# Attention's second-head scaling and output copies moved from VectorE to ScalarE in tiles 0 and 1 of a fused attention and two-MLP kernel

## The chip, the cores and the metric

The kernel runs on one core of a Trainium2 chip. The metric is device time in microseconds, the median of several runs. Engines are named as in the profile: PE (TensorE matmuls), PEld (its weight loads), DVE (VectorE), ACT (ScalarE), POOL (GpSimd), SP (SyncE, which here only issues transfers).

## What is computed

Attention over 4 batches, 8 heads, 512 local and 32 global positions with 64 features a head; local queries see the 32 global keys and a window of 32 keys to either side. Two MLPs follow on the 2176 x 512 result (the weights have 2048 and 1536 hidden columns).

```python
s_ll = np.where(mask, scale * q_l @ k_l.T, -1e9)      # mask: |i - j| <= 32
a_l = sm(concat([scale * q_l @ k_g.T, s_ll]))         # sm: softmax over keys
out_l = a_l @ concat([v_g, v_l])
out_g = sm(scale * q_g @ k_all.T) @ v_all
x = concat([out_g, out_l]) as (tokens, 512)
h = x @ w_in
x = where(h >= 1, h, where(h <= -1, 0, (h + 1)**2 / 4)) @ w_out
out = ((x @ w_a) * (x @ w_b)) @ w_out2
```

## The kernel before

Tokens are worked in six tiles (`TILES`). Tiles 0 to 4 hold three blocks of 128 local queries each, tile 5 the last block and the global queries. One attention **item** (`Local`) is one block and one pair of heads, so a tile of three blocks has 12 items. An item goes through these steps, and the line numbers are those of the profile:

- `s_pe` (L186): scores of the two heads on PE into PSUM. Tiles 0 and 1 (blocks 0 to 5, `stk` false) multiply plain fp32; later blocks (`stk` true) split the operands first (`prep`, L166 to L169).
- `s_post` (L199, L203): DVE adds the mask and finds the row minimum, ACT takes the exponential of each head and its row sum.
- `norm` (L207 to L210): DVE adds 1e-9 to the sums and inverts them; ACT scales the first head's probabilities (L209), DVE the second head's (L210).
- `t_pe`, `t_post` (L216, L220): four PE transposes into one PSUM tile `tp`, which ACT copies to `pt`.
- `v_pe`, `v_post` (L226, L230): eight PE matmuls with the values into PSUM tile `o`, and DVE copies `o` to a slice of `xraw`, the tile's input to the MLP.

`att_atoms` runs the items as a pipeline: step k takes the scores of item k, `norm` of k-1, the transposes of k-2, the values of k-3. All 12 items of tile 0 run first, alone. This is **the opening**. Every eighth piece of it, one weight of the first MLP is converted (`w_conv`, L97 on ACT and L98 to L100 on DVE; `split`, L107 on ACT and L108 on DVE). Four weights are converted in the opening, and the first two steps of tile 1's pipeline fall into it too.

After it `x_split` makes `xh` (ACT, L405) and `xl` (DVE, L406) of tile 0, and the first MLP starts. For each of 16 hidden slices of a tile `h_unit` multiplies into PSUM `hp` (L423 to L425), ACT and DVE make `r`, `m`, `g` (L703 to L709), and `x_unit` accumulates into four `acc` banks. During **tile 0's MLP** (in the profile about 44 to 150 us) the 12 items of tile 1 run between these units, and the other 28 weights of the first MLP are converted. In the MLPs of tiles 1 to 3 the next tile's items and the second MLP's weights are worked; the second MLP comes last.

Work is written in this order, but it is a scheduling pass that places each engine's instructions into its queue; each engine then runs its own queue strictly in order, and waits on semaphores. `e`, `mn` and `sm` have four buffers, PSUM's eight banks are split into four of tag `h` (scores, `hp`) and four of tag `acc` (`tp`, `o` of tile 0, `acc`).

Of the kernel before, what the change touches and what calls it, by code (L numbers as in the profile page):

```python
# [14 lines left out]
AF = mybir.ActivationFunctionType  # L15
# [4 lines left out]
P = 128  # L20
# [38 lines left out]
def body(tc, qk, qkd, vw, kg, vg, w1i, w1o, w2a, w2b, w2o, mask, out):  # L59
    nc = tc.nc  # L60
# [75 lines left out]
    xraw_cur = {}  # L136
# [6 lines left out]
    class Local:  # L143
# [62 lines left out]
        def norm(self):  # L206
            nc.vector.tensor_scalar_add(self.sm, self.sm, 1e-9)  # L207
            nc.vector.reciprocal(self.sm, self.sm)
            nc.scalar.activation(self.e[:, 0], self.e[:, 0], AF.Copy, scale=self.sm[:, 0:1])  # L209
            nc.vector.tensor_scalar_mul(self.e[:, 1], self.e[:, 1], self.sm[:, 1:2])  # L210

        def t_pe(self):
            self.tp = ps.tile([P, 4, P], F32, name="tp", tag=self.tag)
# [13 lines left out]
                                     self.pt[:KC, 2 * c + h], start=c == 0, stop=c == 1)  # L227

        def v_post(self):
            nc.vector.tensor_copy(xraw_cur[self.t][self.p][:, self.j * P:(self.j + 1) * P], self.o)  # L230

    class Gap:
        stk = False
# [674 lines left out]
```

## Time and profile before

| | us |
|---|---|
| median of 3 runs | 957.22 |
| lowest and highest | 955.91, 957.3 |
| the profiled execution | 954.88 |
| its span, first to last instruction | 953.1 |

| stretch of the profiled execution | us |
|---|---|
| first exponential on ACT to the first `xh` (the opening) | 5.36 to 37.21 |
| TensorE clock at its lower level | about 37.0 to 43.6 |
| tile 0's MLP at full clock, tile 1's items in it | 44 to 150 |
| tiles 1 to 3 | 150 to about 430 |

Busy time of an engine counts the time in which at least one of its instructions runs. Back to back instructions of ACT and DVE overlap a little, so what one costs in a full queue is the distance to the next one's start, not its own duration. A wait names what ended it last. The chain of waits follows the work that ended last backwards.

### The profile page before, as it was taken

How to read it: one execution, taken by the hardware profiler on the slowest of the kernel's cores; microseconds unless marked ns; L12 is line 12 of the kernel's file. 1: busy time of each engine (PE TensorE's matmuls, PEld its weight loads, DVE VectorE, ACT ScalarE, POOL GpSimd, SP SyncE). 2: the span in 40 equal slices, each digit the busy share in tenths (PEclk: the TensorE clock that was granted, in tenths of full speed). 3: DMA queues.
4: the chain of work that ended last, by engine and by line, in shares of the span. 5: the costliest groups of instructions: out<-in, count | busy, mean ns of one | idle time of the engine just before them, and what ended most of it. 6: DMA issues, size and time to landing. Idle time of an engine off the chain costs nothing.

```text
span 953.1 us, 16713 instructions
## 1 busy us (share of the span) xinstructions
PE 926.9 (97%) x5964; PEld 840.3 (88%) x5964; DVE 728.2 (76%) x1881; ACT 539.6 (57%) x1293; POOL 0.7 (0%) x7
## 2 busy tenths in 40 slices
PE   7898988999999999999999999999999999999997
PEld 5587777999999999987889999999999999999996
DVE  6799999888877877764348968888896666877663
ACT  8867767666666666654445555555654444654441
POOL 0000000000000000000000000000000000000000
PEclk9899999999999999999999999999999999999999
DMA  7455546444544444333454323321241111131201
GB/s 238 148 189 182 182 164 188 156 133 142 178 142 132 160 156 147 96 120 104 134 194 149 94 79 112 98 69 48 72 147 45 45 45 48 44 121 56 57 12 56
DMA packets 55843, 111.49 MB, mean 117 GB/s; under 512 B 6864, under 2 KB 23376, under 8 KB 55760
## 3 DMA queue, kind: packets, MB, share of 16 engines
q1 hardware_dynamic: 55616, 110.26, 36.4%
q8 instruction: 47, 0.77, 0.3%
q14 instruction: 36, 0.29, 0.1%
q10 hardware_dynamic: 144, 0.17, 0.1%
HBM read 95.20 MB, written 15.20 MB: 116 GB/s over the span
## 4 chain that ended last, share of the span: by engine, by line
PE 84%; DVE 9%; ACT 3%; DMA 2%; issue 1%; SPq 0%; ACTq 0%; DVEq 0%
PE hp L423 6%; PE hp L425 6%; PE hp L424 6%; PE acc L423 6%; PE acc L424 5%; PE acc L425 5%; PE pb L580 5%; PE pb L581 5%; PE py L645 5%; PE pb L578 5%; PE py L646 5%; PE py L644 5%; PE px L578 4%; PE px L581 4%; PE px L580 4%; PE o L226 3%
## 5 line engine op out<-in xcount | busy, mean ns | idle before, releaser
L423 PE MATMUL hp<-xh,w 128*128 128x384 f32 (+1 forms) x384 | 131.5, 342 | 5.4 <-ACT xh L405 2.1
L423 PE MATMUL acc<-g,w 128*128 128x384 f32 (+1 forms) x384 | 132.0, 344 | 4.2 <-ACT g L708 3.6
L424 PE MATMUL acc<-g,w 128*128 128x384 f32 (+1 forms) x384 | 127.1, 331 | 0.0
L425 PE MATMUL hp<-xl,w 128*128 128x384 f32 (+1 forms) x384 | 126.5, 330 | 0.0
L424 PE MATMUL hp<-xh,w 128*128 128x384 f32 (+1 forms) x384 | 126.0, 328 | 0.0
L425 PE MATMUL acc<-g,w 128*128 128x384 f32 (+1 forms) x384 | 125.0, 330 | 0.0
L107 ACT ACTIVATE w<-wt 128x512 fp32r<-128x512 f32 (+1 forms) x116 | 64.9, 564 | 70.8 <-PE pb L581 44.9
L580 PE MATMUL pb<-w 128*128 128x384 f32 (+1 forms) x288 | 94.7, 329 | 0.0
L581 PE MATMUL pb<-w 128*128 128x384 f32 (+1 forms) x288 | 94.3, 327 | 0.0
L578 PE MATMUL pb<-w 128*128 128x384 f32 (+1 forms) x288 | 93.7, 325 | 0.0
L704 DVE SCALAR_TENSOR_TENSOR m<-hp,r 128x384 f32<-128x384 f32 (+1 forms) x96 | 51.1, 532 | 49.5 <-ACT r L703 49.4
L703 ACT ACTIVATE r<-hp,half 128x384 f32<-128x384 f32 (+1 forms) x96 | 53.4, 556 | 61.1 <-PE hp L425 60.6
L423 PEld LDWEIGHTS hp<-xh,w 128*128 128x128 f32 x384 | 72.9, 190 | 12.8 <-issue 3.4
L423 PEld LDWEIGHTS acc<-g,w 128*128 128x128 f32 x384 | 72.4, 189 | 12.5 <-issue 5.3
L645 PE MATMUL py<-w,g 128*128 128x512 f32 x204 | 80.8, 396 | 0.0
L646 PE MATMUL py<-w,g 128*128 128x512 f32 x204 | 80.7, 396 | 0.0
L644 PE MATMUL py<-w,g 128*128 128x512 f32 x204 | 79.6, 390 | 0.0
L108 DVE TENSOR_TENSOR w<-wsum,w 128x256 fp32r<-128x256 f32 (+1 forms) x108 | 54.6, 507 | 29.6 <-ACT w L107 29.6
L424 PEld LDWEIGHTS acc<-g,w 128*128 128x128 f32 x384 | 72.6, 189 | 1.6 <-issue 1.0
L425 PEld LDWEIGHTS acc<-g,w 128*128 128x128 f32 x384 | 72.2, 188 | 1.7 <-issue 1.2
L708 ACT ACTIVATE g<-m 128x384 fp32r<-128x384 f32 (+1 forms) x96 | 48.3, 503 | 44.6 <-DVE m L705 43.9
L425 PEld LDWEIGHTS hp<-xl,w 128*128 128x128 f32 x384 | 72.9, 190 | 0.7 <-DVE xl L406 0.5
(112 smaller groups left out, 2131.6 us busy)
## 6 DMA issues: line engine op xcount, KB each, us to landing
wt<-wd SPq DMA_DIRECT2D x72, 256.0 KB, 2.7
qkd<-in_qkd_dram SPq DMA_DIRECT2D x40, 352.0 KB, 3.1
wraw<-in_w1i_dram SPq DMA_DIRECT2D x16, 512.0 KB, 3.5
wraw<-in_w1o_dram SPq DMA_DIRECT2D x16, 512.0 KB, 4.0
v<-in_vw_dram SPq DMA_DIRECT2D x64, 112.0 KB, 2.8
wraw<-in_w2a_dram SPq DMA_DIRECT2D x12, 512.0 KB, 3.7
wraw<-in_w2b_dram SPq DMA_DIRECT2D x12, 512.0 KB, 4.0
wd<-wt SPq DMA_DIRECT2D x24, 256.0 KB, 2.2
```

The source lines that it names most:

```text
L107: nc.scalar.activation(hi, src, AF.Copy)
L108: nc.vector.tensor_tensor(lo, src, f32(hi), ALU.subtract)
L423: nc.tensor.matmul(acc, whi, xhi, start=first, stop=False)
L424: nc.tensor.matmul(acc, wlo, xhi, start=False, stop=False)
L425: nc.tensor.matmul(acc, whi, xlo, start=False, stop=last)
L578: nc.tensor.matmul(out[:, :n], w[:, 0, r], hi[:, c, :n], start=start and c == 0, stop=False, skip_group_check=True)
L580: nc.tensor.matmul(out[:, :n], w[:, 1, r], hi[:, c, :n], start=False, stop=False, skip_group_check=True)
L581: nc.tensor.matmul(out[:, :n], w[:, 0, r], lo[:, c, :n], start=False, stop=k in (1, 5, 6) and c == 1, skip_group_check=True)
L644: nc.tensor.matmul(a, gh[:, c], w[:, 0], start=f == 0, stop=False)
L645: nc.tensor.matmul(a, gh[:, c], w[:, 1], start=False, stop=False)
L646: nc.tensor.matmul(a, gl[:, c], w[:, 0], start=False, stop=f == NF2 - 1)
L703: at["act"] = nc.scalar.activation(r[:, :W], hp[:, :W], AF.Relu, bias=half, scale=0.5 / W_UP).ins
```

## The change

In `norm` the second head's scaling, and in `v_post` the copy of `o` to `xraw`, go to ACT where `stk` is false, that is for all 24 items of tiles 0 and 1. Later items keep DVE. Nothing else in the code differs.

```diff
@@ norm
             nc.scalar.activation(self.e[:, 0], self.e[:, 0], AF.Copy, scale=self.sm[:, 0:1])
-            nc.vector.tensor_scalar_mul(self.e[:, 1], self.e[:, 1], self.sm[:, 1:2])
+            if self.stk:
+                nc.vector.tensor_scalar_mul(self.e[:, 1], self.e[:, 1], self.sm[:, 1:2])
+            else:
+                nc.scalar.activation(self.e[:, 1], self.e[:, 1], AF.Copy, scale=self.sm[:, 1:2])
@@ v_post
-            nc.vector.tensor_copy(xraw_cur[self.t][self.p][:, self.j * P:(self.j + 1) * P], self.o)
+            x = xraw_cur[self.t][self.p][:, self.j * P:(self.j + 1) * P]
+            if self.stk:
+                nc.vector.tensor_copy(x, self.o)
+            else:
+                nc.scalar.activation(x, self.o, AF.Copy)
```

In the changed file the scaling on ACT is L213, `pt` is L223, the copy on ACT L237, `xh` L412, `hp` L430 to L432, and `m` L711 and L712. The scheduling pass places all queues anew up to the start of tile 1's MLP; behind it they stand as before.

ACT's queue, the end of the opening before: `e` are probabilities, `mn` and `sm` row minima and sums, `xh_625` is the first input of the MLP.

```order
L220 ACTIVATE pt<-tp 112x512
L203 ACTIVATE e,sm<-e,mn 128x224
L107 ACTIVATE w<-wt 128x512
L203 ACTIVATE e,sm<-e,mn 128x224
L209 ACTIVATE e<-e,sm 128x224
L220 ACTIVATE pt<-tp 112x512
L405 ACTIVATE xh_625<-xraw_223 128x384
```

The same place after:

```order
L223 ACTIVATE pt<-tp 112x512
L107 ACTIVATE w<-wt 128x512
L237 ACTIVATE xraw_225<-o 128x128
L203 ACTIVATE e,sm<-e,mn 128x224 x2
L209 ACTIVATE e<-e,sm 128x224
L213 ACTIVATE e<-e,sm 128x224
L223 ACTIVATE pt<-tp 112x512
L237 ACTIVATE xraw_226<-o 128x128
L412 ACTIVATE xh_625<-xraw_223 128x384
```

Each turn of the pipeline now has a second scaling (L213) and an output copy (L237) in ACT's queue, and the last copy stands ahead of `xh`. The queue up to `xh` holds the same 30 exponentials, 13 `pt` copies and four weights (L97, L107) as before, and in addition 14 scalings and 12 copies.

DVE's queue in tile 0's MLP before, from the inversion of one item's sums: `wt`, `wraw` and `w` belong to a weight's conversion, `m`, `g` and `hp` to the MLP.

```order
L207 TENSOR_SCALAR sm<-sm 128x2
L108 TENSOR_TENSOR w<-wt,w 128x512
L208 RECIPROCAL sm<-sm 128x2
L709 TENSOR_TENSOR g<-m,g 128x384
L210 TENSOR_SCALAR e<-e,sm 128x224
L230 COPY xraw_770<-o 128x128
L98 TENSOR_SCALAR wt<-wt 128x512 x2
L99 SCALAR_TENSOR_TENSOR wt<-wraw,wt 128x512 x2
L100 SCALAR_TENSOR_TENSOR wt<-wraw,wt 128x512 x2
L704 SCALAR_TENSOR_TENSOR m<-hp,r 128x384
```

The same place after:

```order
L207 TENSOR_SCALAR sm<-sm 128x2
L108 TENSOR_TENSOR w<-wt,w 128x512
L208 RECIPROCAL sm<-sm 128x2
L716 TENSOR_TENSOR g<-m,g 128x384
L98 TENSOR_SCALAR wt<-wt 128x512
L711 SCALAR_TENSOR_TENSOR m<-hp,r 128x384
L99 SCALAR_TENSOR_TENSOR wt<-wraw,wt 128x512
L98 TENSOR_SCALAR wt<-wt 128x512
```

The item's scaling (L210) and copy (L230) are gone from DVE's queue, and `m` of the next `hp` (L704, now L711) stands behind one conversion instruction where it stood behind six.

## Rows read from the trace of the kernel before

**Rows 1.** Page, parts 1 and 4: busy per engine; the chain by engine.
```profile
PE 926.9 (97%) x5964; PEld 840.3 (88%) x5964; DVE 728.2 (76%) x1881; ACT 539.6 (57%) x1293; POOL 0.7 (0%) x7
...
PE 84%; DVE 9%; ACT 3%; DMA 2%; issue 1%; SPq 0%; ACTq 0%; DVEq 0%
```

**Rows 2.** Stretches: busy us (instructions) of each engine, granted TensorE clock, DMA.
```profile
core 0: us, PE busy (x) PEld busy (x) DVE busy (x) ACT busy (x) POOL busy (x), PEclk, DMA share, GB/s
5.36:37.21 31.85, 26.99 (x218) 18.32 (x216) 27.95 (x131) 30.78 (x96) 0.00 (x0) 1.00 0.75 229
...
44.00:150.00 106.00, 96.23 (x574) 81.47 (x574) 103.38 (x255) 72.06 (x157) 0.00 (x0) 1.00 0.54 178
150.00:240.00 90.00, 88.36 (x579) 81.33 (x579) 75.25 (x221) 62.20 (x164) 0.00 (x0) 1.00 0.48 153
```

**Rows 3.** Chain of waits in the opening, 5 to 37.3 us: shares by line.
```profile
by line: DMA qk<-in_qk_dram 16.6%; PE s L186 15.0%; DVE e L199 10.7%; PE tp L216 10.4%; PE o L226 9.2%; DVE wt L99 5.5%; DVE xraw L230 5.1%; issue 4.2%; DVE e L210 4.1%; DVE wt L100 3.9%; DVE w L108 3.7%; PE warm L191 2.0%; DVE wt L98 2.0%;
```

**Rows 4.** ACT groups, opening: count, busy us, mean ns, idle before.
```profile
L203 ACT ACTIVATE e<-e,mn 128x224 f32<-128x224 f32 x30 | 14.1, 470 | 3.4 <-DVE mn L199 3.2
L220 ACT ACTIVATE pt<-tp 112x512 f32<-112x512 f32 x13 | 7.5, 578 | 0.0
L209 ACT ACTIVATE e<-e,sm 128x224 f32<-128x224 f32 x14 | 6.6, 475 | 0.4 <-DVE sm L208 0.3
L203 ACT ACTIVATION_READ_ACCUMULATOR e<-e,mn 128x1 f32 x30 | 5.7, 189 | 0.0
L97 ACT ACTIVATE wt<-wraw 128x512 f32<-128x512 f32 x4 | 2.6, 666 | 0.0
L107 ACT ACTIVATE w<-wt 128x512 fp32r<-128x512 f32 x4 | 2.5, 622 | 0.2
```

**Rows 5.** ACT timeline, one item and a half: start, duration.
```profile
23.07 0.47 ACT L209 ACTIVATE e<-e,sm 128x224 f32<-128x224 f32 x1
23.45 0.58 ACT L220 ACTIVATE pt<-tp 112x512 f32<-112x512 f32 x1
23.92 0.48 ACT L203 ACTIVATE e<-e,mn 128x224 f32<-128x224 f32 x1
24.30 0.20 ACT L203 ACTIVATION_READ_ACCUMULATOR e<-e,mn 128x1 f32 x1
24.39 0.48 ACT L203 ACTIVATE e<-e,mn 128x224 f32<-128x224 f32 x1
```

**Rows 6.** ACT groups of the whole span: PSUM copies of other sizes.
```profile
L728 ACT ACTIVATE x<-acc 128x384 f32<-128x384 f32 x12 | 5.6, 488 | 2.5 <-PE acc L425 2.5
L728 ACT ACTIVATE x<-acc 128x256 f32<-128x256 f32 x4 | 1.3, 390 | 0.0
L300 ACT ACTIVATE ptg<-tpg 32x128 f32<-32x128 f32 x8 | 2.1, 265 | 4.9 <-PE og L309 4.8
```

**Rows 7.** DVE timeline in the opening: the two operations that are moved.
```profile
15.25 0.33 DVE L210 TENSOR_SCALAR e<-e,sm 128x224 f32<-128x224 f32 x1
15.50 0.29 DVE L230 COPY xraw<-o 128x128 f32<-128x128 f32 x1
15.70 0.38 DVE L199 CUSTOM_DVE_ANT_0 e<-s,masks 128x224 f32<-128x224 f32 x1
```

**Rows 8.** DVE groups, 44 to 150 us.
```profile
L100 DVE SCALAR_TENSOR_TENSOR wt<-wraw,wt 128x512 int32<-128x512 int32 x29 | 19.5, 686 | 0.0
L210 DVE TENSOR_SCALAR e<-e,sm 128x224 f32<-128x224 f32 x10 | 3.3, 332 | 0.0
L230 DVE COPY xraw<-o 128x128 f32<-128x128 f32 x12 | 3.3, 284 | 0.0
```

**Rows 9.** Chain that ended last: first and last moved pieces on it.
```profile
71.28 0.24 DVE e L210
71.53 0.20 DVE xraw L230
...
125.22 0.20 DVE xraw L230
```

**Rows 10.** Waits, 44 to 150 us: us in total, times, longest.
```profile
ACT wt L97 <- DMA wraw<-in_w1o_dram: 4.4, 5, 1.7
PE acc L423 <- ACT g L708: 3.3, 3, 1.7
PE hp L423 <- DVE m L704: 2.0, 3, 1.0
```

**Rows 11.** PE timeline: one item, and the end of the opening.
```profile
27.05 0.65 PE L216 MATMUL tp<-ident,e 128*112 128x128 f32 x4
27.62 0.66 PE L226 MATMUL o<-pt,v 112*64 112x128 f32 x8
28.21 0.65 PE L186 MATMUL s<-qk 64*128 64x224 f32 x4
28.79 0.65 PE L216 MATMUL tp<-ident,e 128*112 128x128 f32 x4
...
34.97 0.66 PE L226 MATMUL o<-pt,v 112*64 112x128 f32 x8
37.77 0.69 PE L423 MATMUL hp<-xh,w 128*128 128x384 f32 x1 [2.14 <-ACT xh L405]
```

**Rows 12.** Stretches of 1 us around the opening's end; the clock is PEclk.
```profile
36.00:37.00 1.00, 0.00 (x0) 0.00 (x0) 0.94 (x3) 1.00 (x4) 0.00 (x0) 0.99 0.54 111
37.00:38.00 1.00, 0.23 (x1) 0.23 (x2) 0.59 (x2) 1.00 (x3) 0.00 (x0) 0.50 0.95 386
43.00:44.00 1.00, 1.00 (x4) 0.50 (x2) 0.00 (x0) 0.58 (x2) 0.00 (x0) 0.60 0.00 0
```


## Prediction

> **What bounds the kernel now.** I read the page first. PE is busy 97% of the span and the chain of waits is 84% PE [rows 1], so an edit on DVE and ACT can only show where PE stands still. That is before 150 us. The table of stretches divides this part in two [rows 2].
>
> In the opening, from the first exponential to the first `xh`, ACT is busy 30.78 of 31.85 us, DVE 27.95, PE 26.99. ACT idles 1.07 us in all: it is the bound, although the chain there walks mostly over transfers, PE and DVE [rows 3]. A chain names one predecessor at each step, and with three engines this full it can walk on any of them; what decides is who has no time left. The MLP can't start before `xh`, and `xh` stands at the end of ACT's queue.
>
> In tile 0's MLP, 44 to 150 us, it is turned round: DVE is busy 103.38 of 106 us, PE 96.23, ACT 72.06 [rows 2]. DVE's load is mostly weight conversion: L100 alone has 29 instructions and 19.5 us [rows 8]. PE has 9.8 us of idle time there, some of it waiting for DVE's `m` (2.0 us) or for `g`, which follows `m` (3.3 us) [rows 10]. From 150 us on DVE falls to 84% and PE is at 98% (75.25 and 88.36 of 90 us) [rows 2], and no queue is changed there; what is won or lost earlier is carried to the end.
>
> So the edit takes work from the bound of the second stretch and gives it to the bound of the first.
>
> **The opening, more work for ACT.** ACT's queue up to `xh` gets 14 scalings (12 items of tile 0 and the first two of tile 1) and 12 copies; all else in it is the same in number. A scaling on ACT is seen: L209 has 475 ns mean [rows 4], but in a full queue the next instruction starts 0.38 us after it (23.07 to 23.45) [rows 5]. 14 x 0.38 = 5.3 us. A 128x128 copy from PSUM on ACT is not in the trace. The nearest rows are 128x384 at 488 ns, 128x256 at 390 ns and 32x128 at 265 ns [rows 6]. 98 ns less for 128 columns less gives 292 ns for one alone; with the overlap of 0.1 us that [rows 5] show it takes 0.19 us in a full queue. 12 x 0.19 = 2.3 us. Alone, behind a wait for PE, it would be 12 x 0.29 = 3.5 us. I take the full queue, since ACT is the engine that is late: the values of item k-3 stand in PE's queue right behind the transposes of k-2, and both wait for scalings that ACT did a turn earlier. Together 7.6 us, 8.8 with copies alone.
>
> What of it can hide? Only ACT's 1.07 us of idle time. The floor is 7.6 - 1.1 = 6.5 us, and it is a hard one as long as instructions keep their durations: 30.78 + 7.6 = 38.4 us of work have to go through ACT before `xh`. I take 7.5, idle time as now, because the waits at the start (for the first scores, whose `qk` transfers are the same) and the round trips remain. DVE loses 14 scalings and 12 copies in the opening, 0.25 and 0.20 us each by the distances of [rows 7], some 5.9 us, and this buys nothing: DVE wasn't last.
>
> The Trainium skill ("ScalarE: Activation LUTs", Rules for kernel authors) advises VectorE over ScalarE for adds and multiplications, which speaks against this change. The rows agree: a scaling takes 0.38 us of ACT's queue [rows 5] and 0.25 us of DVE's [rows 7]. The same page (What ACT_TABLE_LOAD costs) gives 186 ns + 0.833 ns an element for an ACTIVATE with constants, less 93 ns back to back; by that, as an estimate, a copy is 0.20 us and the 12 are 2.4 in place of 2.3 us, and no run here shows it for 128 columns yet.
>
> **Tile 0's MLP, less work for DVE.** All 12 copies of tile 1 and 9 of its scalings fall here (10 L210 are in the stretch, one belongs to tile 2) [rows 8]: 12 x 0.20 + 9 x 0.25 = 4.65 us off an engine that is 97.5% busy. Upper bound of the gain: 4.65 us, all of it. Lower bound: only the moved pieces on which the chain of waits walks, which are six from 71.28 to 125.22 us and sum to 1.5 us [rows 9]. Neither is nearer: DVE is full, but PE with 96.23 of 106 us is the next bound close behind, and where PE ends a wait, DVE's time is worth nothing. I take the middle, 3.1 us. ACT gets 9 x 0.38 + 12 x 0.19 to 0.29 = 5.7 to 6.9 us there, on 72.06 of 106 us. That is hidden by its idle time. If it isn't, it is because a copy that waits for `o` at the head of ACT's queue keeps `r`, `g` and the next weight's L97 waiting behind it; that would eat the gain, down to zero.
>
> **The clock at the seam.** The granted clock is 0.99 at 36 to 37 us, 0.50 from 37 on and back in the 44th microsecond [rows 12], after PE had worked its last values at 34.97 and then waited 2.14 us for `xh` [rows 11]. So 6.6 us run at 1.2 GHz in place of 2.4, and cost about 3.3 us, before and presumably after: the wait for `xh` stays, as two exponentials, two scalings, a `pt` and a copy still stand between the last values and `xh`. I put the change at 0, between -3.3 (it doesn't fall) and +1.4. The latter is a second fall inside the opening. One item's transposes, values and scores take PE 0.58 us each by the starts of [rows 11], 1.75 us together, at half clock 3.5; ACT then needs 38.4 / 14 = 2.74 us an item. In 6.6 us PE would do 1.9 items where ACT could do 2.4, half an item or 1.4 us lost.
>
> "TensorE: Matmul & The Clock Gate" (Part 1: The HAM clock gate) of the Trainium skill says that an idle PE loses its full clock and a busy one gets it back. This trace shows both at the seam; by that rule the longer opening, with PE at 27 of some 39 us, would be more open to a second fall, which is the +1.4 above.
>
> **The sum.** +7.5 - 3.1 + 0 = +4.4 us. The profiled execution took 954.88 us with a span of 953.1, so it would become 959.3. It lies 2.3 us under the median of the runs; on that median, 957.22 us, I predict **961.6 us**.
>
> **Rivals.**
> - *Tile 0's MLP gives back all that the opening takes* (not slower). The place is DVE's queue from 44 to 150 us. If DVE alone is the bound, it is worth 4.65 us and the 2.6 us for which DVE idles now, since the new order puts `m` ahead of conversions: 7.3 us against 7.5, so 957.4 us. For it: DVE's 97.5%, and PE's 9.8 us of idle time, enough room. Against it: PE would have to run at 97% there, with items and MLP competing. It decides if the stretch from the first `hp` to tile 1's MLP gets shorter by over 6 us. Chance 0.13.
> - *The clock doesn't fall at the seam.* 957.2 + 4.4 - 3.3 = 958.3 us. For it: the wait that precedes the fall depends on a few instructions. Against: PE idles more in the new opening, not less. Chance 0.07.
> - *ACT isn't the bound in the opening*, its added work hides and only DVE's gain remains: 957.2 - 3.1 = 954.1 us, faster. The chain, which walks little over ACT there, speaks for it; 1.07 us of idle time against 7.6 us of work speaks against it. Chance 0.06.
> - *Nothing is given back, and the copies wait.* Opening +8.8, a second fall of the clock +1.4, MLP 0: 967.4 us. Chance 0.12.
>
> **How the numbers follow.** The forecast has 0.62: with 6.5 to 8.8 for the opening and 1.5 to 4.65 given back it runs from 959.1 to 964.5. Opening at its floor, full gain and part of the clock's gain reach down to 957.0; opening at 8.8, 1.5 given back and a second fall reach up to 965.9. That is the range, and it leaves out the faster case and the upper end of the heavy one. A change of 0.2%, 1.9 us, is about what a measurement of this kernel can tell from none. Slower by more than that: the forecast and the heavy case, 0.74, less a little for the forecast's lower edge, 0.72. Faster: 0.07. The rest, the give-back and the clock, is within 0.2%: 0.21.
>
> **What would show it.** Right: the first `xh` at 43.7 to 46 us in place of 37.21; ACT over 95% busy ahead of it with DVE at about 22 us of work; copies on ACT near 0.29 us long. In tile 0's MLP, DVE's busy time some 4.7 us less, and the stretch from the first `xh` to the start of tile 1's MLP shorter by 1.5 to 4.7 us. Wrong: `xh` before 42 us, which would say that ACT had room or that its instructions run faster; or a stretch behind it that is shorter by more than 6 us; or a clock that stays at 1.00 around the seam; or half clock for long inside the opening.

## The result and the profile after

| | before | after |
|---|---|---|
| median, us | 956.57 | 968.75 |
| lowest and highest, us | 954.97, 957.3 | 966.7, 971.21 |
| ratio | | 1.013, 95% interval 1.0102 to 1.0158 |
| the profiled execution, its span, us | 954.88, 953.1 | 966.7, 964.9 |

The kernel became slower by 12.2 us, where 4.4 were forecast. The two profiled executions differ by 11.8 us in span, and their traces place the difference so ("MLP" is the time from the first `xh` to DVE's first copy of a finished `acc` bank of tile 0, L730 before and L737 after, to 0.04 us):

| us | before | after | difference | forecast |
|---|---|---|---|---|
| first `xh` | 37.21 | 48.42 | +11.2 | +7.5 |
| tile 0's MLP | 108.74 | 109.51 | +0.8 | -3.1 |
| the rest | 807.15 | 806.97 | -0.2 | 0 |

Stretches of the trace after, which answer [rows 2]: busy time (instructions) of each engine, granted clock, DMA. They are the opening, the clock's low stretch behind it, and the rest of tile 0's MLP:

```profile
core 0: us, PE busy (x) PEld busy (x) DVE busy (x) ACT busy (x) POOL busy (x), PEclk, DMA share, GB/s
5.67:48.42 42.75, 35.49 (x218) 23.07 (x216) 22.92 (x104) 37.59 (x121) 0.00 (x0) 0.80 0.56 175
48.42:55.50 7.08, 6.49 (x17) 4.75 (x18) 3.71 (x9) 4.50 (x12) 0.00 (x0) 0.53 0.03 11
55.50:157.93 102.43, 93.79 (x560) 78.87 (x559) 95.87 (x222) 75.28 (x170) 0.00 (x0) 1.00 0.54 173
```

The same two parts of the MLP in the trace before:

```profile
37.21:44.00 6.79, 6.23 (x16) 4.56 (x16) 3.55 (x9) 3.82 (x10) 0.00 (x0) 0.51 0.17 66
44.00:145.95 101.95, 92.74 (x558) 79.03 (x557) 99.50 (x242) 69.56 (x150) 0.00 (x0) 1.00 0.53 174
```

Three things are to be seen. First, in the opening ACT is busy 6.8 us longer than in [rows 2], but the opening is 10.9 us longer, and ACT now idles 5.2 us. Second, the granted clock there is 0.80, where it was 1.00. Third, in the MLP DVE loses 3.6 us of work (99.50 to 95.87), and yet the stretch doesn't get shorter: it takes 102.43 us in place of 101.95.

**The clock in the opening.** "Half clock" is time at TensorE's lower level, 1.2 GHz in place of 2.4, which the rows show as 0.50. Stretches of 1 us of the trace after:

```profile
23.00:24.00 1.00, 0.13 (x4) 0.00 (x0) 0.23 (x2) 1.00 (x3) 0.00 (x0) 1.00 0.82 252
24.00:25.00 1.00, 0.27 (x1) 0.30 (x2) 0.00 (x0) 1.00 (x4) 0.00 (x0) 0.65 0.80 239
...
34.00:35.00 1.00, 1.00 (x10) 0.72 (x10) 0.11 (x1) 1.00 (x5) 0.00 (x0) 0.73 0.47 145
...
41.00:42.00 1.00, 0.19 (x3) 0.12 (x2) 0.56 (x4) 1.00 (x4) 0.00 (x0) 0.69 0.00 0
...
54.00:55.00 1.00, 1.00 (x3) 0.55 (x3) 0.00 (x0) 0.34 (x1) 0.00 (x0) 0.50 0.00 0
```

The rows between the first two and the third, and between the fourth and the fifth, stand at 0.50. Twice the shortfall of each row from 1.00 gives the time at the lower level: 10.2 us in the first spell, 13.6 in the second, 17.3 of the 23.9 ahead of the first `xh`. Before, [rows 12] had one spell of 6.8 us in all, behind the opening. PE's timeline shows how the first spell begins:

```profile
22.47 0.66 PE L229 MATMUL o<-pt,v 112*64 112x128 f32 x8
24.73 1.08 PE L186 MATMUL s<-qk 64*128 64x224 f32 x2 [1.60 <-DMA qk<-in_qk_dram]
25.74 1.10 PE L219 MATMUL tp<-ident,e 128*112 128x128 f32 x4
```

PE waits 1.60 us for a `qk` transfer, and then the four transposes that took 0.65 us in [rows 11] take 1.10. Who suffers is in the waits of 5.67 to 48.42 us (us in total, times, longest):

```profile
DVE e L199 <- PE tp L219: 8.0, 4, 3.7
...
ACT w L107 <- DVE wt L100: 3.6, 2, 1.9
```

and in the timelines of DVE and of ACT in that spell:

```profile
26.98 0.39 DVE L199 CUSTOM_DVE_ANT_0 e<-s,masks 128x224 f32<-128x224 f32 x1 [3.72 <-PE tp L219]
...
28.67 0.69 DVE L100 SCALAR_TENSOR_TENSOR wt<-wraw,wt 128x512 int32<-128x512 int32 x1
```

```profile
29.39 0.63 ACT L107 ACTIVATE w<-wt 128x512 fp32r<-128x512 f32 x1 [1.92 <-DVE wt L100]
29.93 0.26 ACT L237 ACTIVATE xraw<-o 128x128 f32<-128x128 f32 x1
```

DVE stands 3.72 us before an item's mask: PE stood still for 1.60 us of it, for the transfer, and then did the scores and the transposes at half clock. The weight's conversion (L98 to L100) stands behind that mask in DVE's queue, so it comes late, and ACT, which does L107 between two items, stands 1.92 us before it with an output copy and the next exponentials queued behind. The same happens once more three us behind the spell, with the clock full again:

```profile
37.42 0.63 ACT L107 ACTIVATE w<-wt 128x512 fp32r<-128x512 f32 x1 [1.68 <-DVE wt L100]
```

So 3.6 of ACT's 5.2 us of idle time are at L107. What they show is a late PE that takes time from an ACT that has none to give. How much of the lateness is the clock, the transfer or the order of the queues, these waits alone don't say.

**What the moved instructions cost.** ACT's groups in 5.67 to 48.42 us, beside [rows 4], and two rows of its timeline:

```profile
L213 ACT ACTIVATE e<-e,sm 128x224 f32<-128x224 f32 x14 | 6.7, 476 | 0.0
...
L237 ACT ACTIVATE xraw<-o 128x128 f32<-128x128 f32 x12 | 3.2, 268 | 0.4 <-PE o L229 0.4
L107 ACT ACTIVATE w<-wt 128x512 fp32r<-128x512 f32 x4 | 2.5, 629 | 3.6 <-DVE wt L100 3.6
```

```profile
13.64 0.26 ACT L237 ACTIVATE xraw<-o 128x128 f32<-128x128 f32 x1
13.80 0.47 ACT L209 ACTIVATE e<-e,sm 128x224 f32<-128x224 f32 x1
```

A copy takes 268 ns (292 were estimated) and 0.16 us of a full queue (0.19 estimated). The scalings are as [rows 4] and [rows 5] had L209. The copies hardly wait for `o`: 0.4 us in all.

### The profile page after: what moved, and what is told of

The parts are those of the page before. It is cut to its first block, busy times and chain, and to the rows that moved or that the text cites. A ratio compares the mean times of both kernels' runs of the same rounds, so it can differ in the third digit from the quotient of the medians.

```text
span 964.9 us, 16733 instructions
## 1 busy us (share of the span) xinstructions
PE 936.5 (97%) x5964; PEld 844.9 (88%) x5964; DVE 719.5 (75%) x1833; ACT 553.2 (57%) x1341; POOL 0.7 (0%) x7
## 3 DMA queue, kind: packets, MB, share of 16 engines
q1 hardware_dynamic: 55616, 110.26, 36.3%
## 4 chain that ended last, share of the span: by engine, by line
PE 84%; ACT 5%; DVE 5%; DMA 4%; issue 1%; SPq 0%; ACTq 0%; DVEq 0%
PE hp L430 6%; PE acc L430 6%; PE acc L431 6%; PE hp L432 6%; PE hp L431 6%; PE acc L432 5%; PE pb L587 5%; PE pb L588 5%; PE py L652 5%; PE pb L585 5%; PE py L653 5%; PE py L651 5%; PE px L585 4%; PE px L587 4%; PE px L588 4%; PE o L229 3%
## 5 line engine op out<-in xcount | busy, mean ns | idle before, releaser
L430 PE MATMUL acc<-g,w 128*128 128x384 f32 (+1 forms) x384 | 131.2, 343 | 5.7 <-ACT g L715 4.9
L430 PE MATMUL hp<-xh,w 128*128 128x384 f32 (+1 forms) x384 | 131.5, 342 | 3.5 <-ACT xh L412 2.1
L432 PE MATMUL hp<-xl,w 128*128 128x384 f32 (+1 forms) x384 | 126.7, 330 | 0.0
L432 PE MATMUL acc<-g,w 128*128 128x384 f32 (+1 forms) x384 | 124.9, 330 | 0.0
L107 ACT ACTIVATE w<-wt 128x512 fp32r<-128x512 f32 (+1 forms) x116 | 65.1, 564 | 70.0 <-PE pb L588 44.9
L711 DVE SCALAR_TENSOR_TENSOR m<-hp,r 128x384 f32<-128x384 f32 (+1 forms) x96 | 51.1, 532 | 48.4 <-ACT r L710 48.2
L430 PEld LDWEIGHTS acc<-g,w 128*128 128x128 f32 x384 | 72.3, 189 | 12.8 <-ACT g L715 6.9
L430 PEld LDWEIGHTS hp<-xh,w 128*128 128x128 f32 x384 | 72.9, 190 | 11.0 <-issue 3.6
L431 PEld LDWEIGHTS acc<-g,w 128*128 128x128 f32 x384 | 72.5, 189 | 3.0 <-issue 2.0
L108 DVE TENSOR_TENSOR w<-wt,w 128x512 fp32r<-128x512 f32 (+1 forms) x116 | 70.0, 606 | 6.4 <-ACT w L107 5.0
L432 PEld LDWEIGHTS hp<-xl,w 128*128 128x128 f32 x384 | 72.9, 190 | 0.8 <-DVE xl L413 0.7
```

The lines of the kernel that those rows point to most:

```text
L107: nc.scalar.activation(hi, src, AF.Copy)
L108: nc.vector.tensor_tensor(lo, src, f32(hi), ALU.subtract)
L430: nc.tensor.matmul(acc, whi, xhi, start=first, stop=False)
L431: nc.tensor.matmul(acc, wlo, xhi, start=False, stop=False)
L432: nc.tensor.matmul(acc, whi, xlo, start=False, stop=last)
```

## The experiments

Two questions had to be told apart. Where do the opening's 11.2 us come from: ACT's added work, or PE's lower clock, or the `qk` transfer that sets it off? And is DVE the bound of tile 0's MLP, so that work taken from it is won? The table has all runs. Half clock is worked out from rows of 1 us as above. The ratio is to the kernel before, run beside each; the rounds ran on different chips, so kernels of different rounds are compared by their ratios. The columns from the first `xh` on come from one profiled execution of each kernel; "fill" is explained below.

| kernel | median us | ratio (95%) | first `xh` | half clock ahead of it | MLP | half clock in it | DVE busy in it |
|---|---|---|---|---|---|---|---|
| before | | | 37.21 | 0.2 | 108.74 | 6.6 | 103.05 |
| after | 968.75 | 1.0130 (1.0102 to 1.0158) | 48.42 | 17.3 | 109.51 | 6.6 | 99.58 |
| tile 0 alone | 967.74 | 1.0116 (1.0090 to 1.0143) | 45.70 | 12.4 | 113.00 | 11.5 | 102.81 |
| tile 1 alone | 957.47 | 1.0009 (0.9993 to 1.0026) | 38.41 | 0 | 112.69 | 13.6 | 99.65 |
| after, `qk` earlier | 968.41 | 1.0118 (1.0089 to 1.0148) | 45.59 | 9.3 | 115.81 | 21.5 | 99.83 |
| after, fill | 960.69 | 1.0041 (1.0023 to 1.0058) | 43.38 | 0 | 108.35 | 6.8 | 99.62 |
| tile 0 alone, fill | 958.23 | 1.0023 (1.0011 to 1.0035) | 43.35 | 0 | 106.00 | 0 | 102.58 |
| before, fill | 954.97 | 0.9986 (0.9970 to 1.0001) | 34.46 | 0 | 111.19 | 3.4 | 105.22 |
| tile 1 alone, fill | 951.48 | 0.9953 (0.9936 to 0.9969) | 36.04 | 0 | 107.80 | 3.4 | 100.84 |
| scalings alone, fill | 959.68 | 1.0037 (1.0024 to 1.0050) | 38.19 | 0 | 110.75 | 6.8 | 103.69 |
| tile 1's scalings | 958.83 | 1.0030 (1.0001 to 1.0060) | 38.15 | 0 | 113.41 | 17.0 | 101.68 |
| tile 1's copies | 955.75 | 1.0010 (0.9985 to 1.0035) | 38.07 | 0 | 108.13 | 3.4 | 100.97 |
| before, tile 1 unscaled | 954.94 | 0.9995 (0.9975 to 1.0015) | 37.63 | 0.1 | 111.60 | 13.6 | 103.13 |
| before, tile 1's copies twice | 957.66 | 1.0020 (0.9996 to 1.0043) | 43.97 | 10.2 | 110.59 | 10.2 | 104.29 |

What comes after the MLP takes 806.2 to 808.0 us in all of them but one (tile 1 unscaled, 804.7), so nearly all is decided in these columns.

**The clock from run to run.** Each run lists its span and its granted clock, and twice the shortfall of the clock, times the span, is its half clock. The four runs of the changed kernel have 25 to 39 us of it, and the profiled one the least; the 73 runs of the kernel before that were made beside the experiments (one run of 5072.84 us left out) have 3.8 to 23.0 us. Among these 73, each round taken against its own mean, each us of half clock goes with 0.42 us more of time (correlation 0.84). The queues are the same in all of them, so their order has no part in this. It is a reading and not an experiment: the pauses of PE that set the clock off are in it too.

**Which tile.** The change in tile 0 alone (`self.t != 0`) and in tile 1 alone (`self.t != 1`):

```diff
-            if self.stk:
+            if self.t != 0:
                 nc.vector.tensor_scalar_mul(self.e[:, 1], self.e[:, 1], self.sm[:, 1:2])
...
-            if self.stk:
+            if self.t != 0:
                 nc.vector.tensor_copy(x, self.o)
```

> The change in tile 0 alone (the opening and the items that start in it keep DVE in tile 1). Theory A (in the changed kernel the opening pays 11.2 us, because the clock falls inside it, and tile 0's MLP gives nothing back): the first xh near 48 us, 966 to 968 us. Theory B (the sum on record: tile 0's MLP would give back 3.1 us, something else in the changed kernel cancelled it): then leaving tile 1 on DVE costs more than the whole change, 970 to 972 us. If the opening's extra 3.7 us come from the two steps of tile 1 that fall into it, the xh comes at 43 to 45 us and the time is 963 to 964 us.

> The change in tile 1 alone; up to the first xh PE's order is that of the kernel before. Theory A (DVE loses 4.3 us of work but waits as much longer for ACT): the first xh near 37.2 us as before, 956 to 958 us. Theory B (tile 0's MLP is bound by DVE and gives back): 952 to 954 us.

Tile 0 alone makes nearly the whole loss (+1.16%). Its time is that of Theory A, but its `xh` comes at 45.70 and not near 48, and the rest of the loss is in an MLP with 11.5 us of half clock. Tile 1 alone makes no loss that can be told from zero, and no gain, as Theory A had it. Tile 1's trace has 10.2 us of half clock behind the opening and 3.4 later, where before had 6.6.

**Is it the `qk` transfer?** The changed kernel with a fourth `qk` buffer, loaded one item earlier (the loop that issues the loads is changed with it and not shown):

```diff
-                self.qk = sp["q"].tile([P, P + KW], F32, name="qk", bufs=3)
+                self.qk = sp["q"].tile([P, P + KW], F32, name="qk", bufs=4)
```

> The changed kernel with four buffers for the scores' inputs in place of three, each loaded one item earlier. If the first fall of the clock is set off by the one wait of PE for such a load (1.6 us, at 23 us): no wait for it, the clock holds beyond 30 us and the first xh comes 1.5 to 3.5 us earlier, 965 to 967 us. If PE's emptier opening is enough for the fall without it: the clock falls all the same, 968 to 969 us.

After 9 us no wait for `qk` is left, and the first spell is gone; the clock held until about 36.3 us. Then it fell all the same, as the stretch of 1 us there shows, in a pause of PE of 1.33 us for a scaling on ACT (L209), behind a microsecond with PE at 0.44:

```profile
36.00:37.00 1.00, 0.23 (x1) 0.23 (x2) 0.53 (x3) 1.00 (x5) 0.00 (x0) 0.66 0.69 250
```

It stayed low until about 57 us. The `xh` came 2.8 us earlier, the MLP with 21.5 us of half clock was 6.3 us longer, and the time is that of the changed kernel. So the first spell began at the late transfer, but without it the loss is the same: an opening that ACT has made longer leaves PE with pauses enough.

**The clock held by fill.** The kernel has idle matmuls of the identity (`warm`, L191), two in each of the first four items. Here they go on through all items of the opening, four from the fifth item on, and compute nothing that is used (`fill` takes the number as an argument; that line is not shown):

```diff
-NWARM, WARM_ITEMS = 2, 4
+NWARM, WARM_ITEMS = 2, 15
...
-                    it.fill()
+                    it.fill(NWARM if k < 4 else 4)
```

> The changed kernel with four more idle matmuls on PE in each item of the opening from the fifth on (0.14 us each at full clock), so that PE idles less; they compute nothing that is used. Theory A (the half clock inside the opening holds PE up and through it ACT): the granted clock stays at 1.00 up to the last items, ACT's idle time in the opening falls from about 5 us to under 2, the first xh comes at 44 to 46 us and the time is 964 to 966 us. Theory C (ACT's idle time comes from the new order of the queues, not from the clock): the xh stays at 48 to 49 us or comes later, 968 to 971 us.

> The change in tile 0 alone with four idle matmuls in each item of the opening from the fifth on. Set against the changed kernel with the same (960.7 us), this is the give-back once more, from the other side. Theory A: 960 to 961.5 us. Theory B: 963 to 965 us. The first xh at 43 to 44 us in both.

Stretches from 5 us to the first `xh` and from there to the MLP's end, with the change in tile 0 alone, without and with fill:

```profile
5.00:45.70 40.70, 34.06 (x220) 22.01 (x218) 24.37 (x109) 36.59 (x119) 0.00 (x0) 0.85 0.63 188
45.70:158.70 113.00, 102.06 (x573) 85.44 (x573) 102.81 (x250) 73.57 (x159) 0.00 (x0) 0.95 0.49 159
```

```profile
5.00:43.35 38.35, 36.67 (x310) 27.98 (x306) 24.95 (x109) 36.49 (x120) 0.00 (x0) 1.00 0.63 197
43.35:149.35 106.00, 96.66 (x573) 81.70 (x573) 102.58 (x250) 73.41 (x159) 0.00 (x0) 1.00 0.52 172
```

ACT and DVE do the same work in both, the clock differs, and the spans of these two executions differ by 9.9 us (966.2 and 956.3); the ratios differ by 0.93%, 8.9 us. The changed kernel with fill in the opening:

```profile
5.00:43.38 38.38, 37.28 (x310) 28.59 (x308) 24.18 (x106) 37.18 (x122) 0.00 (x0) 1.00 0.65 201
```

With the clock held, ACT is busy 37.18 of 38.38 us and `xh` stands at 43.38, 6.2 us later than before. That is ACT's own work. The other 5.0 us, to 48.42, went when the clock held. Both times came out lower than any theory had them: 960.69 where Theory A had 964 to 966, and 958.23 where 960 to 961.5 were the lowest. Four idle matmuls took 1.0 us of PE an item, and not four times 0.14.

One caution: fill doesn't change the clock alone. The scheduling pass places the queues anew around the idle matmuls, and ahead of `xh` the scores on PE, the masks among DVE's conversions and the scalings on ACT stand in another order than without it; ACT has no wait at L107 left. So Theory C, the order, isn't ruled out by these two runs. Two things speak for the clock with the order unchanged: the runs of the kernel before, above, and a pair of executions below.

**Fill without the change, and with tile 1's half.** Two idle matmuls an item here (the first line of the diff above alone):

> The kernel before with two idle matmuls on PE in every item of the opening (there are two in the first four items already); they compute nothing that is used. Theory A (each microsecond of half clock at the seam costs half a microsecond): the clock holds past the first xh, and of the 6.6 us at half clock up to 3.3 us are saved, 953.5 to 955.5 us. Rival (tile 0's MLP is bound by DVE's work, so that PE's lost time at its start is hidden): 956.5 to 958 us though the clock holds.

> The change in tile 1 alone, with the same two idle matmuls in each item of the opening. Set against the kernel before with them, in both the clock should hold, so this shows what tile 0's MLP gives back without the clock. Theory A (DVE waits for ACT in place of working): within 1 us of it. Theory B (it gives back 3.1 us): 2.5 to 4 us less.

```profile
5.00:34.46 29.46, 29.05 (x230) 21.04 (x226) 26.25 (x116) 27.70 (x85) 0.00 (x0) 1.00 0.78 242
34.46:145.65 111.19, 102.49 (x613) 85.92 (x609) 105.22 (x269) 76.21 (x170) 0.00 (x0) 0.98 0.53 167
```

```profile
5.00:36.04 31.04, 28.72 (x228) 20.59 (x224) 26.21 (x116) 27.63 (x84) 0.00 (x0) 1.00 0.74 232
36.04:143.84 107.80, 100.74 (x616) 85.71 (x612) 100.84 (x246) 82.81 (x194) 0.00 (x0) 0.98 0.53 172
```

The first pair is the kernel before with fill, the second tile 1's half with fill. The second is the fastest kernel of all, 951.48 us, 0.47% under before and 0.33% under before with fill; its MLP is 3.4 us shorter at the same half clock, with 4.4 us less on DVE. Its `xh` comes 1.6 us later, though, and what follows the MLP is 1.4 us shorter, so the line between the parts has moved as well. The gain is what Theory B had (2.5 to 4 us). Whether it is DVE's relief or the new order of the queues was not separated. Before with fill gains next to nothing, although `xh` comes 2.75 us earlier, because it comes earlier by leaving work for later: the scheduling pass has put 26 exponentials ahead of it where [rows 4] have 30, and the MLP is 2.45 us longer.

**Scalings without copies, with the stronger fill.** (`if True` ahead of DVE's copy.)

> Only the scalings go to ACT, in both tiles, with four idle matmuls in each item of the opening from the fifth on. If the opening is ACT's queue and nothing else, 14 scalings of 0.37 us less the idle time that they fill put the first xh at 41.3 to 42.4 us, 1.2 to 2 us ahead of both edits together (43.4 us), and the time at 958.7 to 959.7 us. If copies that wait for PE cost ACT more than their own 0.16 us each, the xh comes at 40.5 us or earlier and the time is 957 to 958.5 us.

```profile
L203 ACT ACTIVATE e<-e,mn 128x224 f32<-128x224 f32 x26 | 12.2, 472 | 3.4 <-DVE mn L199 3.4
L223 ACT ACTIVATE pt<-tp 112x512 f32<-112x512 f32 x11 | 6.3, 577 | 0.0
```

The `xh` at 38.19 is that of the second theory and the time of 959.68 that of the first. ACT's groups ahead of `xh` show why this says little: four exponentials and two `pt` copies fewer than in [rows 4]. With the distances of [rows 5], 0.47 us each, and one scaling of each head they make 3.6 us, and 38.19 + 3.6 = 41.8 is within what was expected of the scalings. The total is inconclusive on the copies.

**DVE's load in the MLP, one piece at a time.** Tile 1's scalings alone, its copies alone, and two kernels that touch DVE only: before with tile 1's second-head scaling left out, so that these heads are not normalized, and before with tile 1's copies done twice. The last two are shown:

```diff
-            nc.vector.tensor_scalar_mul(self.e[:, 1], self.e[:, 1], self.sm[:, 1:2])
+            if self.t != 1:
+                nc.vector.tensor_scalar_mul(self.e[:, 1], self.e[:, 1], self.sm[:, 1:2])
```

```diff
             nc.vector.tensor_copy(xraw_cur[self.t][self.p][:, self.j * P:(self.j + 1) * P], self.o)
+            if self.t == 1:
+                nc.vector.tensor_copy(xraw_cur[self.t][self.p][:, self.j * P:(self.j + 1) * P], self.o)
```

> Only tile 1's second-head scalings go to ACT; its copies and all of tile 0 stay on DVE. Of tile 1's 12 scalings 2 fall into the opening and 9 into tile 0's MLP before 150 us. DVE-bound theory (what leaves DVE's queue in tile 0's MLP is won): opening +0.8, MLP -9 x 0.25 = -2.3, together -1.5 us. Other theory (DVE, ACT and PE wait for each other there by turns, and DVE's time alone is worth nothing): +0.8 us, between 0 and +2.

> Only tile 1's copies of o go to ACT; all scalings and tile 0 stay on DVE. All 12 copies lie in tile 0's MLP, so the opening stays as before. DVE-bound theory: -12 x 0.20 = -2.4 us. Other theory: 0, or up to +2 where a copy that waits for o at the head of ACT's queue keeps the weight conversion waiting.

> The kernel before without tile 1's second-head scalings: they are left out on DVE and not done on ACT, so that tile 1's second heads are not normalized. DVE loses 12 x 0.25 = 3.0 us, 9 or 10 of them in tile 0's MLP, and ACT gets nothing. DVE-bound theory: -2.3 to -3 us. Other theory: -1 to +1 us. If this gains and the scalings on ACT alone don't, it is ACT's added work in the MLP that eats the gain.

> The kernel before with each of tile 1's 12 copies of o done twice on DVE, so 12 x 0.20 = 2.4 us more on DVE in tile 0's MLP and nothing else. DVE-bound theory: +2.4 us, and DVE's idle time from 44 us on stays at 2.5 us. Other theory: within +1 us, taken from that idle time.

By the DVE-bound theory these should have given -1.5, -2.4, -2.3 to -3 and +2.4 us. Their ratios make it +2.9, +1.0, -0.5 and +1.9, each with an interval of 2 to 3 us to either side. The one that matters most is the kernel with 3 us of DVE's work left out and nothing given to ACT: -0.5, and its interval (0.9975 to 1.0015) reaches to -2.4, which leaves the theory only its lowest value. Its trace tells more: what follows the MLP is 2.5 us shorter than before, but the MLP is 2.9 us longer, with 7.0 us more of half clock. The doubled copies can't tell the theories apart.

The clock of each run helps a little further. Taking 0.42 us off for each us of half clock, an estimate by the 73 runs above, the kernel without these scalings comes out 2.1 us under before on the mean, the scalings on ACT 1.1 us over it, the copies on ACT 1.5 over and the copies done twice 1.2 over. By this reading DVE's time was worth something where ACT got nothing to do for it, and ACT's added work ate it. It rests on a price per us that varies from kernel to kernel, so it is an indication.

**The clock with the queues unchanged.** The profiled execution of the kernel with tile 1's copies done twice took 963.88 us, 6.2 us over the median of that kernel. Up to the first `xh` nothing was changed in it, and PE, ACT and DVE do the same instructions in the same order as in the trace before. PE's timeline has these rows:

```profile
9.77 1.06 PE L216 MATMUL tp<-ident,e 128*112 128x128 f32 x4
...
20.93 0.65 PE L186 MATMUL s<-qk 64*128 64x224 f32 x4 [1.52 <-DMA qk<-in_qk_dram]
21.51 0.66 PE L216 MATMUL tp<-ident,e 128*112 128x128 f32 x4
22.10 1.12 PE L226 MATMUL o<-pt,v 112*64 112x128 f32 x8
```

and its first two stretches, as above, are

```profile
5.00:43.97 38.97, 33.88 (x220) 22.07 (x216) 28.56 (x133) 31.23 (x96) 0.00 (x0) 0.87 0.62 195
43.97:154.56 110.59, 101.24 (x576) 85.32 (x576) 104.29 (x262) 72.66 (x158) 0.00 (x0) 0.95 0.48 163
```

`xh` stands at 43.97 with ACT busy 31.23 us; in the three kernels beside it, with ACT at 30.5 to 31.0 us, it stood at 37.63 to 38.15. As the order is the same, each instruction can be set against its own start in the trace before. PE is 0.3 us behind at 9.77, and 2.75 us behind at 15.4: up to there the transposes take 1.06 us, as at half clock, although the rows of the granted clock read 1.00 so early. The late transfer at 20.93 brings this to 3.2 us. At the end of the half clock, at 32.4, it is 7.7 us. A pause of 1.1 us that the kernel before has next takes up some of it, and `xh` is 6.8 us late. So most of the delay came while PE was slow, and little from the transfer.

**Tile 0's MLP over all 14 traces.** The best straight line through the table's columns is 107.0 us plus 0.40 us for each us at half clock, with a scatter of 1.2 us. With DVE's busy time as a second column it is 0.42 us, and 0.28 us for each us of DVE, with a scatter of 1.1; the standard errors are 0.05 and 0.17. This is a reading over kernels that differ in more than these columns, not an experiment, and a longer pause of PE can be behind both the time and the clock. Half clock goes with most of what this stretch does; what DVE's load is worth can't be told from it.

## Why the prediction was wrong

- **The opening's ACT term held, if a little too large.** Forecast +7.5 with a floor of 6.5 that was called hard; with the clock held by fill it is +6.2 (43.38 against 37.21), with ACT busy 37.18 of 38.38 us. The copies were 0.03 us cheaper in the queue than estimated, 0.4 us for 12, which is more than `xh` fell short of the floor. The rival "ACT isn't the bound" falls with it.
- **The clock term failed, and it is the larger of two misses.** It was put at 0, with +1.4 at most for a second fall inside the opening. There were 17.3 us of half clock ahead of `xh`, and `xh` came 5.0 us later than with the clock held; the different order of the queues under fill is in this figure. At 0.42 us for each us, from the 73 runs, 17.3 us would be 7.3 us, an estimate, so the clock is enough for all of it. The price per us was not far off: the prediction's own rates (3.5 us an item for PE at half clock, 2.74 for ACT) give 17.3/2.74 - 17.3/3.5 = 1.4 items, 3.8 us. What failed was the length, taken as the 6.6 us of the seam, and the place: it was treated as a side case, although the prediction itself noted that PE would be busy 27 of some 39 us. What the sum lacked beside it is the coupling that the waits show, PE to DVE's mask to the conversion to ACT's L107. The profiled execution also had the least half clock of the four runs, so the median has more of it in it than the traces show. The Trainium skill ("TensorE: Matmul & The Clock Gate", Part 1: The HAM clock gate), which the prediction set behind this term, says that an idle PE loses its clock. The rows agree: the first fall came in the pause of 1.60 us.
- **The seam** cost what it did: 6.6 us of half clock behind `xh` in both traces. The rival in which the clock doesn't fall there came true only with fill.
- **The give-back failed.** Forecast -3.1, bounds -1.5 to -4.65; measured +0.8. DVE's load fell by 3.6 of the 4.65 us that were worked out (99.50 to 95.87 us in the rest of the MLP), and its idle time took all of it: 2.45 us before, 6.56 after. The waits of 55 to 161 us, beside [rows 10], say on what (the last line is the kernel before, 44 to 150 us):

```profile
PE acc L430 <- ACT g L715: 4.4, 3, 2.9
DVE w L108 <- ACT w L107: 4.1, 9, 1.2
...
DVE m L711 <- ACT r L710: 2.6, 1, 2.6
...
ACT xraw L237 <- PE o L229: 1.7, 3, 0.8
...
DVE w L108 <- ACT w L107: 0.9, 3, 0.5
```

- DVE now waits 4.1 us for ACT's half of a weight's split, nine times (0.9 us, three times, before), and PE waits 4.4 us for `g` where it was 3.3. A busy share of 97.5% was read as a bound. But conversion goes ACT, DVE, ACT, DVE, and the same ACT got 5.7 us more to do (69.56 to 75.28). That this added work ate the gain fits the waits and the estimate by the runs' clocks above; no run isolates it. The lower end of the term should have been at or past zero: the prediction named how a copy at the head of ACT's queue "would eat the gain, down to zero", and left it out of the bounds.
- **The rivals.** The heavy one (967.4 us) came nearest in time, right in that nothing was given back and the clock fell again, and by luck in the number: the copies didn't wait (0.4 us in all), and the clock cost more than its 1.4. "Gives back all" (957.4) fell with the MLP at +0.8 us.
- **By the terms:** 6.2 (ACT's work) + 5.0 (clock, with the order under fill in it) + 0.8 (MLP) - 0.2 (rest) = 11.8 us, the difference of the spans. The changed kernel with fill is 0.41% over before, 3.9 us and near the forecast 4.4, but that doesn't bear out the sum: its opening costs 6.2 us where 7.5 were forecast, and its MLP gives back 0.4 us where 3.1 were.

What stays open is what tile 1's half is worth in the MLP by itself. With fill it gained 3.2 us of span against before with fill; on top of tile 0's half with fill it lost 2.3 us, and there the MLP has 6.8 us of half clock in one case and none in the other. That late spell begins in a pause of PE near the end of tile 0's MLP, for `g`, here in the changed kernel with fill and then in the fastest kernel:

```profile
133.17 0.69 PE L430 MATMUL acc<-g,w 128*128 128x384 f32 x1 [2.94 <-ACT g L715]
```

```profile
124.43 0.69 PE L430 MATMUL acc<-g,w 128*128 128x384 f32 x1 [3.44 <-ACT g L715]
```

Where such a pause falls changes with every new order of the queues, and no trace here with work of tile 1 moved to ACT kept full clock through the MLP: the idle matmuls need a PSUM bank of tag `acc`, and in the MLP all four are in use.

## What to carry to other kernels

Work that is moved to an engine with no time left costs its distances in that queue, and this was worked out to about 1 us here (7.5 forecast, 6.2 with the clock held); ask next what the longer stretch does to TensorE's granted clock, and price the whole stretch at the lower level if PE is not full there, through every engine that waits for PE. A busy share near 100% on an engine that hands work to and fro with another is no proof that its time can be won: look at how often each waits for the other, and give the gain a lower end of zero. Where the clock is at stake, a version with idle matmuls shows what the work costs at full clock; compare the order of the queues before the rest is put down to the clock. The clocks and times of many runs of one kernel give the clock's price with the order unchanged. With two idle matmuls an item, the half of the change that was harmless became a gain of 0.47%.

## What the runs showed of the hardware

- Half clock is dear even where PE is not the only bound: 0.42 us for each us over 73 runs of the kernel before. Tile 0 alone, without and with fill, agrees: 23.9 us of half clock and 9.9 us of span in the two traces, 0.41 us for each us, with the order of the queues different too.
- With the queues unchanged, 10.2 us of half clock in the opening put PE from 3.2 to 7.7 us behind (before with the copies twice, against before).
- The rows of the granted clock can miss the start: in that execution they read 1.00 at 9.77 us, where four transposes took 1.06 us; four took 0.66 us at 21.51.
- A 128x128 fp32 copy from PSUM on ACT has 268 ns, and the next ACTIVATE starts 0.16 us after it. The Trainium skill ("ScalarE: Activation LUTs", What ACT_TABLE_LOAD costs) gives 186 ns + 0.833 ns an element less 93 back to back, 293 and 200 ns as an estimate; the rows are some 10 and 20% lower.
- The clock fell in or soon behind a pause of PE: in the changed kernel in one of 1.60 us (PE was busy 0.13 and 0.27 of the two microseconds from 23 to 25), in that with `qk` earlier in one of 1.33 us (0.44 and 0.23 from 35 to 37), and in the execution with the late transfer at about 22 us, when PE was at work again behind a pause of 1.52 us.
